# Retention with a gated mixture of attention experts on one core: a tile's value products moved half a step to a step later, the loads of its transposed weights to the head of the step, and its scaling and transposes in among the projections' copies

## The chip, the cores and the metric

The kernel runs on one core of one Trainium2 chip. The metric is the time of one execution on the device, in microseconds (us); the median of several runs is compared.

## What is computed

The first half is a retention layer without softmax, the second a layer of four attention experts of which each token uses two:

```
q, k, v: (8, 8, 576, 64) fp32                                  # batch, heads, tokens, head size
ret[b,h] = (0.125 * q @ k^T * D_h) @ v                          # D_h[i,j] = gamma_h ** (i-j) for i >= j, else 0
x = ret, heads side by side: (8, 576, 512)
w = softmax of the two largest of x @ w_gate (512 x 4)          # per token
for e in 0..3:                                                  # experts, head size 64
    a = causal softmax of 0.125 * (x @ wq[e]) @ (x @ wk[e])^T
    out += w[:, e] * (a @ (x @ wv[e]) @ wo[e])                  # only where e is one of the two
```

## The kernel before

**Steps.** The tokens of a batch are cut into five chunks (`CH`: 128, 128, 128, 128 and 64 rows), so there are 40 chunks (`NC`), and the main loop goes through 42 steps n. Everything is issued in the order in which the code is written: the schedule is manual for all engines, so each engine has one queue in program order and an instruction that waits holds up all that stands behind it. What a step does depends on n mod 5; below, "kind 3" is a step with n mod 5 = 3, and so on.

In step n the kernel (a) issues the loads of chunk n+2 (`load`); (b) does the retention of chunk n: `qk`, the carried state `state`, and with one step of delay `result(n - 1)`, whose matrix products are `old` and `own` and whose elementwise rest (`late`) runs on GpSimd and ScalarE; (c) scores tile m = n - 6 of the second half (`scores`: TensorE products `ss`, then per expert a masked minimum `nm` on VectorE and an exponential on ScalarE); (d) `gates` after a batch's half has its gate logits, `decay` for the next chunk; (e) `normal(m)`: reciprocal row sums on VectorE, then four scalings on ScalarE (L374; two for a tile of kind t = 4); (f) `spread(m)`: VectorE transposes 32x32 blocks (L383) and one DMA writes them to a buffer `hb` in HBM (L386); (g) `work(n)`: projections `pj` (q and k), `pv` (v and gate logits) and `po` (output) of whichever batch is due, by the table `STEPS`; (h) `gather(m)`: four DMAs bring the blocks back as `pth`, now fully transposed (L394); (i) `values(m - 1)`: the products `ys` of the transposed weights with v (L429), copied by ScalarE (`y`, L442) and split into two fp32r parts on GpSimd.

So a tile of place t in its batch (t = 0..4, growing wider with t because of the causal mask) is scored in the step of kind t + 1 (t = 4: kind 0), and its `ys` stands at the end of the next step. Tiles t = 2 and 3 have `pth` loads of 768 KB and 1 MB.

**The table of work.** By n mod 5: kind 3 has the first-half q and k projections (`kq0`, 48 matmuls), kind 4 the output projection `o0` of the batch before (24), kind 0 the values `v0` (24), kind 1 `kq1` (48, wider), kind 2 `o1` and then `v1` (24 and 36).

**PSUM.** All products go to one pool of eight banks (`bank`, tag "b") that are handed out in turn: a new bank waits for the reader of the bank handed out eight before. SBUF has a ring "big" of three buffers for `tr` and the raw weights, and a ring of two for `p32`, the scores.

**DMA.** All transfers are issued by SyncE (SP) in program order, so a `pth` load that waits for its `hb` write to land holds up the loads behind it.

**End.** After step 41 `end()` finishes the last tiles; tiles from LAST + 1 = 36 on are transposed on TensorE (`turn`) instead of through HBM.

Of the kernel before, what the change touches and what calls it, by code (L numbers as in the profile page):

```python
# [34 lines left out]
def kernel(ctx: ExitStack, tc: tile.TileContext, xf, xt, vkf, vkt,  # L35
# [167 lines left out]
    def fetch(n):  # L203
        o, kc, w = WCUT[n]
        RAW[n] = raw = ld.tile([128, kc, w], F32, name="raw", tag="big", bufs=3)
        nc.sync.dma_start(raw, wraw[:, o:o + kc * w].rearrange("p (k w) -> p k w", k=kc))
# [99 lines left out]
    def scores(m):  # L306
# [18 lines left out]
        else:  # L325
            ps = []
            for p in range(2):
                ps.append([bank([128, 288], "ss") for j in range(2)])
                for i in range(2):
                    for z in range(2):  # L330
                        j = i ^ z
                        mm(ps[p][j][HALF[z]], q[p][HALF[z], l0:l0 + C], k[p][HALF[z], 288 * j:288 * j + 288],  # L332
                           start=True, stop=True)
        p32 = sb.tile([128, n, w if t < 4 else 640], F32, name="p32", tag="p32", bufs=2)
        if t == 4:
# [21 lines left out]
    def normal(m):  # L357
        b, t = divmod(m, 5)
        t0, C = CH[t]
        r = 0 if t < 2 else 1  # L360
        ti = t - RNG[r][2][0]
        p32, sm, n = SS[m]
        wt = WT[b, r]
        rs = sm[:, 1, :n]
        v.tensor_scalar(sm[:, 0, :n], sm[:, 0, :n], 1e-9, None, op0=OP.add)
        v.reciprocal(rs, sm[:, 0, :n])
        if t < 4:
            v.tensor_mul(rs, rs, wt[:, ti])  # L368
        else:
            for z in range(2):  # L370
                hr = slice(64 * z, 64 * z + 64)
                v.tensor_mul(rs[hr], rs[hr], wt[hr, ti, z::2])
        for e in range(n):
            act(p32[:, e, :t0 + C], p32[:, e, :t0 + C], AF.Copy, scale=rs[:, e:e + 1])  # L374

    HB = {}

    def spread(m):
        p32, sm, n = SS.pop(m)
        nj = m % 5 + 1  # L380
        tr = ld.tile([128, 4, n, nj, 32], F32, name="tr", tag="big", bufs=3)
        for e in range(n):
            v.transpose(tr[:, :, e].rearrange("p b j c -> p j b c"),  # L383
                        p32[:, e, :128 * nj].rearrange("p (j b c) -> p j b c", b=4, c=32))
        HB[m] = hb = hbm.tile([128, 4, n * nj * 32], F32, name="hb", tag="hb")
# [78 lines left out]
    for b in range(B):  # L464
        late = b == B - 1

        for n, kind in ((5 * b + 3, "kq0"), (5 * b + 5 - late, "v0"), (5 * b + 6, "kq1"), (5 * b + 7, "v1"),
                        (5 * b + 9 + (b == B - 2), "o0"), (5 * b + 12, "o1")):
            if b or kind[-1] == "1" or kind == "o0":
                STEPS.setdefault(n, []).append((b, kind, None))  # L470

# [21 lines left out]

    LAST = NC - 5
    TILES = {n: [n - LAG] for n in range(LAG, NC + 1)}
    TILES[NC].append(LAST)
    TILES[NC + 1] = [LAST + 1]

    def end():
# [6 lines left out]
        gates()  # L506
        normal(LAST + 3)
        run(scores(LAST + 4))
        for d in range(4):
            run(outproj(b - 1, 1, d))  # L510
        run(turn(LAST + 3))
        normal(LAST + 4)
        run(scores(LAST + 2))
        for d in range(4):
            run(outproj(b, 0, d))
        values(LAST + 3)
        run(turn(LAST + 4))
        normal(LAST + 2)
        values(LAST + 4)
        run(turn(LAST + 2))  # L520
# [11 lines left out]
    for n in range(NC + 2):  # L532
# [6 lines left out]
        if n in (1, 4):  # L539
            fetch("v" if n == 1 else "o")  # L540
        new, old = TILES.get(n, []), TILES.get(n - 1, [])
        late = result(n - 1) if 1 <= n <= NC else iter(())
# [15 lines left out]
        soft = scores(new[0]) if new else iter(())  # L558
        turns = (None for m in old if m > LAST for _ in turn(m))
        for i, _ in enumerate(soft):  # L560
            if i:
                next(turns, None)
        if n > 5:
            run(late)
        decay(n + 1)
        run(turns)
# [5 lines left out]
        for m in new:  # L572
            normal(m)
            if m <= LAST:
                spread(m)
        run(work(n))
        for m in new:
            if m <= LAST:
                gather(m)
        run(late)  # L580
        for m in old:
            values(m)
    end()


# [53 lines left out]
```

## Time and profile before

| | |
|---|---|
| median of 3 runs (lowest, highest) | 531.57 us (527.06 to 533.68) |
| profiled execution, its own time | 527.11 us |
| span of that execution, first to last instruction | 525.3 us |
| mean granted TensorE clock | 0.932 |
| TensorE matmul busy | 438.9 us |
| ScalarE / VectorE / GpSimd busy | 298.7 / 291.5 / 214.3 us |
| DMA | 97.38 MB, mean 185 GB/s |

Around the span lie 1.8 us of the profiled time. Durations below come from this one execution. Five steps make one batch; a row of the timeline gives start, duration, engine, line, operation, tiles, shapes and count, and in brackets the idle time of that engine ahead of it with what ended it.

### The profile page before, as it was taken

The page shows a single profiled execution, that of the slowest core. Times are in us where ns is not written, and L with a number is a line of the kernel's source. Part 1 is how long each engine was busy: PE and PEld are TensorE (multiplying, and loading weights), DVE is VectorE, ACT ScalarE, POOL GpSimd, SP SyncE. Part 2 cuts the span into 40 slices and gives each one's busy share as a digit, 9 for nine tenths or more (in the row PEclk, how much of TensorE's full clock was granted, in tenths as well). Part 3 has the DMA queues.
Part 4 walks back from the last instruction along what each step waited for, and adds up shares of the span by engine and source line. Part 5 has one row for each costly group of instructions (what it writes and reads, how often), then busy time and mean ns, then how long its engine had stood idle before and what let it go on. Part 6 is the DMA issues. An engine that isn't in the chain of part 4 may idle for free. (4 is left out here: it accounts for less than half of the span.)

```text
span 525.3 us, 18683 instructions
## 1 busy us (share of the span) xinstructions
PE 438.9 (84%) x7642; PEld 384.2 (73%) x7642; DVE 291.5 (55%) x1050; ACT 298.7 (57%) x886; POOL 214.3 (41%) x285
## 2 busy tenths in 40 slices
PE   6498886699877998789966998689987799587996
PEld 3488775699757896689855997579966798376785
DVE  3646665475744656475655547467565466643451
ACT  2365766356653576447573475645765465836493
POOL 2347444355343443454443453445435354320200
PEclk9599998899977999799998999799998899979899
DMA  8862258756388373865678554875739834456021
GB/s 295 303 201 86 92 182 276 228 158 204 143 265 242 115 235 116 277 210 177 204 237 256 171 176 155 268 230 170 233 118 286 250 116 132 121 161 181 2 81 62
DMA packets 48437, 97.38 MB, mean 185 GB/s; under 512 B 5600, under 2 KB 29408, under 8 KB 47456
## 3 DMA queue, kind: packets, MB, share of 16 engines
q1 hardware_dynamic: 48352, 96.19, 57.7%
q8 instruction: 61, 1.00, 0.8%
q14 instruction: 24, 0.20, 0.1%
HBM read 63.53 MB, written 32.64 MB: 183 GB/s over the span
## 5 line engine op out<-in xcount | busy, mean ns | idle before, releaser
L352 ACT ACTIVATE p<-p,nm 128x128 f32<-128x128 f32 (+4 forms) x144 | 82.9, 578 | 76.4 <-DVE nm L344 57.1
L429 PE MATMUL ys<-pth,vn 128*64 128x128 f32 (+1 forms) x960 | 67.4, 301 | 52.8 <-DMA pth<-hb 36.7
L374 ACT ACTIVATE p<-p,sm 128x128 f32<-128x128 f32 (+4 forms) x144 | 73.0, 575 | 62.7 <-DVE sm L368 51.2
L429 PEld LDWEIGHTS ys<-pth,vn 128*64 128x64 f32 x960 | 57.4, 162 | 59.4 <-DVE tr L383 25.3
L443 POOL CAST yh<-y 128x256 fp32r<-128x256 f32 (+1 forms) x39 | 14.6, 374 | 179.7 <-ACT y L442 179.7
L383 DVE STREAM_TRANSPOSE tr<-p 128x128 f32<-128x128 f32 (+3 forms) x130 | 64.6, 536 | 26.8 <-ACT p L374 17.7
L184 DVE TENSOR_TENSOR x<-x,own 128x256 f32<-128x256 f32 (+1 forms) x80 | 26.4, 363 | 84.5 <-ACT x L169 67.8
L144 POOL TENSOR_SCALAR_AFFINE_SELECT p<-p 64x512 f32<-64x512 f32 (+1 forms) x80 | 49.1, 613 | 30.1 <-ACT p L141 20.6
L344 DVE CUSTOM_DVE_ANT_0 p<-ss,mask 128x512 f32<-128x512 f32 (+3 forms) x128 | 54.9, 484 | 8.9 <-PE ss L323 8.8
L192 POOL TENSOR_TENSOR x1l<-x,x1h 128x512 fp32r<-128x512 f32 (+1 forms) x24 | 26.3, 1097 | 58.3 <-ACT x1h L190 58.3
L189 POOL TENSOR_TENSOR x<-x,gi 128x512 f32<-128x512 f32 (+1 forms) x38 | 44.8, 1180 | 3.4 <-DVE s L126 0.4
L323 PE MATMUL ss<-k,q 64*64 64x512 f32 (+3 forms) x512 | 45.1, 443 | 1.3 <-ACT p L141 0.7
L442 ACT ACTIVATE y<-ys 128x256 f32<-128x256 f32 (+1 forms) x39 | 14.2, 364 | 40.5 <-PE ys L429 40.5
L166 PE MATMUL old<-x,s 64*64 64x64 f32 x1024 | 26.4, 230 | 11.8 <-ACT k L238 10.8
L179 PE MATMUL own<-p,vk 64*64 64x64 f32 x1152 | 29.7, 232 | 5.4 <-issue 3.6
L141 ACT ACTIVATE p<-qk 128x256 f32<-128x256 f32 (+1 forms) x80 | 24.8, 367 | 15.3 <-PE qk L138 15.3
L105 POOL TENSOR_TENSOR vk<-vk,con 128x512 f32<-128x512 f32 (+1 forms) x34 | 32.5, 955 | 0.1
L166 PEld LDWEIGHTS old<-x,s 64*64 64x64 f32 x1024 | 21.8, 144 | 13.4 <-ACT k L238 11.7
L179 PEld LDWEIGHTS own<-p,vk 64*64 64x64 f32 x1152 | 25.8, 145 | 6.1 <-issue 5.2
L138 PE MATMUL qk<-x 64*64 64x64 f32 x1152 | 29.6, 246 | 0.0
L454 PE MATMUL po<-yh,who 128*128 128x320 f32 (+1 forms) x128 | 29.1, 309 | 0.6 <-ACT yh L438 0.6
L138 PEld LDWEIGHTS qk<-x 64*64 64x64 f32 x1152 | 23.9, 154 | 7.5 <-issue 5.5
(113 smaller groups left out, 996.5 us busy)
## 6 DMA issues: line engine op xcount, KB each, us to landing
x<-xf SPq DMA_DIRECT2D x32, 512.0 KB, 5.5
vk<-vkf SPq DMA_DIRECT2D x32, 512.0 KB, 6.3
hb<-tr SPq DMA_DIRECT2D x7, 1024.0 KB, 5.2
pth<-hb SPq DMA_DIRECT2D x28, 256.0 KB, 5.0
hb<-tr SPq DMA_DIRECT2D x7, 768.0 KB, 3.9
pth<-hb SPq DMA_DIRECT2D x28, 192.0 KB, 3.7
out<-ot SPq DMA_DIRECT2D x32, 160.0 KB, 2.7
hb<-tr SPq DMA_DIRECT2D x7, 640.0 KB, 3.8
```

The source lines that it names most:

```text
L105: (gp if n > 5 else v).tensor_mul(vv, vv, gam[:, 2 * c:2 * c + k].unsqueeze(3).to_broadcast([128, k, 4, D]))
L138: mm(ps[g][HALF[r], s, u], x[HALF[g], 1, h, i], x[HALF[g], 0, h, i], start=True, stop=True)
L144: gp.affine_select(w, w, pattern=[[0, 4 * k], [1, 64]], base=0, channel_multiplier=-1, compare_op=OP.is_ge, fill=0.0)
L166: mm(old[g][HALF[u], r, i], S_[b, k - 1][HALF[g], r, u], x[HALF[g], 0, 2 * r + u, i], start=True, stop=True)
L179: mm(own[r][HALF[u], g, i], vk[HALF[r], s, 0, 2 * g + u], p[HALF[r], g, s, u], start=True, stop=True)
L189: e.tensor_mul(x32, x32, gi[:, :, t0:t0 + C])
L323: mm(ps[2 * p + z][HALF[i]], q[p][HALF[z], l0 + 64 * i:l0 + 64 * i + 64], k[p][HALF[z], :w], start=True, stop=True)
L344: v.tensor_tensor_reduce(p32[:, e], ps[e], mask[:, 512 - w:], -1.0, BIG, OP.add, OP.min, nm[:, e:e + 1])
L352: act(p32[:, e, :w], p32[:, e, :w], AF.Exp, bias=bias, scale=-1.0, accum_out=sm[:, 0, e:e + 1])
L374: act(p32[:, e, :t0 + C], p32[:, e, :t0 + C], AF.Copy, scale=rs[:, e:e + 1])
L383: v.transpose(tr[:, :, e].rearrange("p b j c -> p j b c"), p32[:, e, :128 * nj].rearrange("p (j b c) -> p j b c", b=4, c=32))
L429: mm(py[64 * z:64 * z + 64, p], VN[b, rr][0][:, j - 2 * rr, e * D:(e + 1) * D], src, start=(j == 0), stop=(j == t))
```

## The change

It does five things. `values(m)` moves from the end of step m + 7 to the middle of step m + 8, behind the scoring of that step and ahead of `decay`, `gates`, `normal` and `work`. `gather(m)` moves from the end of step m + 6 to the head of step m + 7, behind that step's `load`. The scalings leave `normal` and go into `spread`, which is now a generator: one scaling and one transpose per expert are issued after each piece of `work` from the second on, and the `hb` write after the last of them. The table `STEPS` cuts `kq0` in two, one half each in kinds 3 and 4, and moves `o0` by one step to kind 0; within a step v comes first, then o, then the q and k projections. `p32`, `tr` and the raw weights share one ring of four buffers. At the end the tiles from 34 on (`FAR = LAST - 1`) are transposed on TensorE.

```diff
-        p32 = sb.tile([128, n, w if t < 4 else 640], F32, name="p32", tag="p32", bufs=2)
+        p32 = ld.tile([128, n, w if t < 4 else 640], F32, name="p32", tag="big", bufs=4)
...
-        for e in range(n):
-            act(p32[:, e, :t0 + C], p32[:, e, :t0 + C], AF.Copy, scale=rs[:, e:e + 1])
...
     def spread(m):
-        p32, sm, n = SS.pop(m)
+        t0, C = CH[m % 5]
+        p32, sm, n = SS[m]
         nj = m % 5 + 1
-        tr = ld.tile([128, 4, n, nj, 32], F32, name="tr", tag="big", bufs=3)
+        if m < FAR:
+            tr = ld.tile([128, 4, n, nj, 32], F32, name="tr", tag="big", bufs=4)
         for e in range(n):
-            v.transpose(tr[:, :, e].rearrange("p b j c -> p j b c"),
-                        p32[:, e, :128 * nj].rearrange("p (j b c) -> p j b c", b=4, c=32))
+            act(p32[:, e, :t0 + C], p32[:, e, :t0 + C], AF.Copy, scale=sm[:, 1, e:e + 1])
+            if m < FAR:
+                v.transpose(tr[:, :, e].rearrange("p b j c -> p j b c"),
+                            p32[:, e, :128 * nj].rearrange("p (j b c) -> p j b c", b=4, c=32))
+            yield
+        if m >= FAR:
+            return
+        SS.pop(m)
         HB[m] = hb = hbm.tile([128, 4, n * nj * 32], F32, name="hb", tag="hb")
         nc.sync.dma_start(hb, tr.rearrange("p b e j c -> p b (e j c)"))
...
-        for n, kind in ((5 * b + 3, "kq0"), (5 * b + 5 - late, "v0"), (5 * b + 6, "kq1"), (5 * b + 7, "v1"),
-                        (5 * b + 9 + (b == B - 2), "o0"), (5 * b + 12, "o1")):
+        for n, kind, part in ((5 * b + 3, "kq0", 0), (5 * b + 4 - late, "kq0", 1), (5 * b + 5 - late, "v0", None),
+                              (5 * b + 6, "kq1", None), (5 * b + 7, "v1", None), (5 * b + 10, "o0", None),
+                              (5 * b + 12, "o1", None)):
...
+    for n in STEPS:
+        STEPS[n].sort(key=lambda x: "vok".index(x[1][0]))
...
+    FAR = LAST - 1
...
-        new, old = TILES.get(n, []), TILES.get(n - 1, [])
+        new, old, far = TILES.get(n, []), TILES.get(n - 1, []), TILES.get(n - 2, [])
+        for m in old:
+            if m < FAR:
+                gather(m)
...
         if n > 5:
             run(late)
+        for m in far:
+            if m < FAR:
+                values(m)
         decay(n + 1)
...
         for m in new:
             normal(m)
-            if m <= LAST:
-                spread(m)
-        run(work(n))
-        for m in new:
-            if m <= LAST:
-                gather(m)
+        spreads = (None for m in new for _ in spread(m))
+        for i, _ in enumerate(work(n)):
+            if i:
+                next(spreads, None)
+        run(spreads)
         run(late)
         for m in old:
-            values(m)
+            if m >= FAR:
+                values(m)
```

How the queues read, at three places in the middle of the program. First ScalarE, from the exponentials of a tile t = 2 (step kind 3) to the retention copies of the next step; `p` scaled by `sm` is the scaling, `k` and `q` from `pj` are the copies of the projections, `y` that of the value products. Before:

```order
L352 ACTIVATE p_3302,sm<-p_3302,nm 128x384 x4
L190 ACTIVATE x1h<-x_3227 128x4x128
L294 ACTIVATE ex<-ex 128x12
L374 ACTIVATE p_3302<-p_3302,sm 128x384 x4
L238 ACTIVATE k_3349<-pj 128x256
L240 ACTIVATE q_3351<-pj 128x256
L238 ACTIVATE k_3350<-pj 128x256
L240 ACTIVATE q_3352<-pj 128x256
L442 ACTIVATE y_3423<-ys 128x256
L141 ACTIVATE p<-qk 128x128 x2
L169 ACTIVATE x_3448<-old 128x256 x2
```

ScalarE at the same place now:

```order
L352 ACTIVATE p_3291,sm<-p_3291,nm 128x384 x4
L190 ACTIVATE x1h<-x_3216 128x4x128
L448 ACTIVATE y_3312<-ys 128x256
L294 ACTIVATE ex<-ex 128x12
L383 ACTIVATE p_3291<-p_3291,sm 128x384
L238 ACTIVATE k_3338<-pj 128x256
L383 ACTIVATE p_3291<-p_3291,sm 128x384 x3
L240 ACTIVATE q_3340<-pj 128x256
L141 ACTIVATE p<-qk 128x128 x2
L169 ACTIVATE x_3407<-old 128x256 x2
```

The copy `y` now stands ahead of the gates' exponential, two of the four projection copies have gone to the next step, and one of the other two stands behind the first scaling.

Second TensorE, from the end of a step of kind 4 into one of kind 0; `vn_2101` and `vn_1639` before are the halves of v that tile t = 2 needs. Before:

```order
L454 MATMUL po<-yh_2159,wlo 128x256 x2
L429 MATMUL ys<-pth,vn_1639 64x128 x4
L429 MATMUL ys<-pth,vn_2101 64x128 x2
L429 MATMUL ys<-pth,vn_1639 64x128 x4
L429 MATMUL ys<-pth,vn_2101 64x128 x2
L138 MATMUL qk<-x 64x64 x16
L166 MATMUL old<-x,s 64x64 x8
L179 MATMUL own<-p,vk 64x64 x8
L118 MATMUL st<-vk 64x64 x16
L332 MATMUL ss<-k_1283,q_1842 64x288 x4
L332 MATMUL ss<-k_1284,q_1843 64x288 x4
L257 MATMUL pv<-whv,xh 128x260 x4
```

TensorE now, with the same tile's products:

```order
L233 MATMUL pj<-xh,wlq 128x256 x4
L138 MATMUL qk<-x 64x64 x16
L166 MATMUL old<-x,s 64x64 x8
L179 MATMUL own<-p,vk 64x64 x8
L118 MATMUL st<-vk 64x64 x16
L332 MATMUL ss<-k_1272,q_1831 64x288 x4
L332 MATMUL ss<-k_1273,q_1832 64x288 x4
L435 MATMUL ys<-pth,vn_1592 64x128 x4
L435 MATMUL ys<-pth,vn_2050 64x128 x2
L435 MATMUL ys<-pth,vn_1592 64x128 x4
L435 MATMUL ys<-pth,vn_2050 64x128 x2
L257 MATMUL pv<-whv,xh 128x260 x4
```

The `ys` of tile t = 2 has moved past the retention products and the scores of the next step and stands directly ahead of `pv`.

Third SP's queue, from the loads at the head of a step of kind 3 to the tile t = 3 of kind 4. Before:

```order
L92 DMA x<-xf 128x1024
L96 DMA vk<-vkf 128x1024
L386 DMA hb<-tr 128x1536
L394 DMA pth<-hb 32x4x384 x4
L92 DMA x<-xf 128x1024
L96 DMA vk<-vkf 128x1024
L386 DMA hb<-tr 128x2048
L458 DMA out<-ot 128x256 x4
L394 DMA pth<-hb 32x4x512 x4
```

SP's queue now, from the write of the tile t = 2:

```order
L392 DMA hb<-tr 128x1536
L92 DMA x<-xf 128x1024
L96 DMA vk<-vkf 128x1024
L400 DMA pth<-hb 32x4x384 x4
L392 DMA hb<-tr 128x2048
L92 DMA x<-xf 128x1024
L96 DMA vk<-vkf 128x1024
L400 DMA pth<-hb 32x4x512 x4
L392 DMA hb<-tr 128x1280
```

Each pair of loads `x` and `vk` now stands between a tile's `hb` write and its `pth` loads, and the four `out` writes have left this stretch.

More of the change, by code (lines that the diff above doesn't have):

```diff
@@ L204, in fetch @@
         o, kc, w = WCUT[n]
-        RAW[n] = raw = ld.tile([128, kc, w], F32, name="raw", tag="big", bufs=3)
+        RAW[n] = raw = ld.tile([128, kc, w], F32, name="raw", tag="big", bufs=4)
         nc.sync.dma_start(raw, wraw[:, o:o + kc * w].rearrange("p (k w) -> p k w", k=kc))
@@ L465 @@
         late = b == B - 1
-        for n, kind in ((5 * b + 3, "kq0"), (5 * b + 5 - late, "v0"), (5 * b + 6, "kq1"), (5 * b + 7, "v1"),
-                        (5 * b + 9 + (b == B - 2), "o0"), (5 * b + 12, "o1")):
+        for n, kind, part in ((5 * b + 3, "kq0", 0), (5 * b + 4 - late, "kq0", 1), (5 * b + 5 - late, "v0", None),
+                              (5 * b + 6, "kq1", None), (5 * b + 7, "v1", None), (5 * b + 10, "o0", None),
+                              (5 * b + 12, "o1", None)):
             if b or kind[-1] == "1" or kind == "o0":
-                STEPS.setdefault(n, []).append((b, kind, None))
+                STEPS.setdefault(n, []).append((b, kind, part))
+    for n in STEPS:
+        STEPS[n].sort(key=lambda x: "vok".index(x[1][0]))
     for n, kind, part in ((2, "kq0", 0), (3, "kq0", 1), (4, "v0", 0), (5, "v0", 1)):
@@ L507, in end @@
         normal(LAST + 3)
+        run(spread(LAST + 3))
         run(scores(LAST + 4))
@@ L512, in end @@
         normal(LAST + 4)
+        run(spread(LAST + 4))
         run(scores(LAST + 2))
@@ L518, in end @@
         normal(LAST + 2)
+        run(spread(LAST + 2))
         values(LAST + 4)
@@ L558 @@
         soft = scores(new[0]) if new else iter(())
-        turns = (None for m in old if m > LAST for _ in turn(m))
+        turns = (None for m in old if m >= FAR for _ in turn(m))
         for i, _ in enumerate(soft):
```

## The prediction

> **What bounds the kernel now.** I read first how busy the engines are over the whole span.
>
> ```profile
> PE 438.9 (84%) x7642; PEld 384.2 (73%) x7642; DVE 291.5 (55%) x1050; ACT 298.7 (57%) x886; POOL 214.3 (41%) x285
> ```
>
> TensorE is the fullest engine, and 525.3 - 438.9 = 86 us of it are idle. The view of waits, for TensorE alone, says what ended the idle times (total, times, longest):
>
> ```profile
> PE ys L429 <- DMA pth<-hb: 36.7, 11, 5.1
> PE old L166 <- ACT k L238: 10.8, 7, 1.7
> PE ys L429 <- DVE lg L262: 8.3, 2, 4.2
> PE ys L429 <- DVE tr L383: 7.5, 2, 3.8
> ```
>
> Three of the four are the value products `ys` waiting for their transposed weights: 52.5 us in 15 waits. The names behind the arrow in the third and fourth differ only because several semaphores are waited for; the loads of `pth` follow those transposes. Next, where they sit: one batch in the view by stretches, cut where the scores of a tile start (kinds 3, 4, 0, 1, 2; length, then busy time of the engines, then granted clock, DMA share and GB/s).
>
> ```profile
> 252.84:264.46 11.62, 9.96 (x174) 8.60 (x167) 9.03 (x32) 6.63 (x20) 4.23 (x5) 1.00 0.46 132
> 264.46:277.68 13.22, 9.48 (x176) 7.79 (x169) 6.57 (x19) 9.34 (x26) 7.26 (x10) 0.87 0.90 288
> 277.68:292.50 14.82, 10.36 (x197) 8.83 (x192) 6.93 (x22) 5.36 (x14) 4.67 (x8) 0.88 0.75 218
> 292.50:303.50 11.00, 11.00 (x243) 10.57 (x239) 7.46 (x34) 5.96 (x24) 5.47 (x8) 1.00 0.57 176
> 303.50:315.10 11.60, 11.60 (x227) 10.87 (x220) 5.71 (x25) 8.32 (x26) 6.15 (x8) 1.00 0.53 175
> ```
>
> Two of five stretches (the last two rows) have TensorE busy throughout at full clock, 2.4 GHz; nothing but less TensorE work could shorten them. The idle time lies in the first three, and in the second and third part of the time is at 1.2 GHz. Their waits one by one, in the timeline of TensorE:
>
> ```profile
> 263.42 0.62 PE L166 MATMUL old<-x,s 64*64 64x64 f32 x26 [1.66 <-ACT k L238]
> 273.23 1.95 PE L429 MATMUL ys<-pth,vn 128*64 128x128 f32 x24 [3.74 <-DVE tr L383]
> 277.68 2.11 PE L332 MATMUL ss<-k,q 64*64 64x288 f32 x16
> 287.32 3.22 PE L429 MATMUL ys<-pth,vn 128*64 128x128 f32 x32 [4.46 <-DMA pth<-hb]
> ```
>
> So a batch loses 1.66 us to a bank that the copy of `k` frees late, 3.74 us to tile t = 2 and 4.46 us to tile t = 3. The same three parts over all batches, as sums of stretches of the view: from the scores of t = 2 to those of t = 4 (seven of them), from there to those of t = 0 (six), on to those of t = 2 (six); and the whole middle, six cycles of five steps:
>
> ```profile
> sum 179.70, PE 138.97 PEld 116.93 DVE 108.45 ACT 110.26 POOL 77.22; mean PE 19.85 PEld 16.70 DVE 15.49 ACT 15.75 POOL 11.03
> sum 80.50, PE 60.50 PEld 51.68 DVE 41.77 ACT 32.75 POOL 28.82; mean PE 10.08 PEld 8.61 DVE 6.96 ACT 5.46 POOL 4.80
> sum 137.80, PE 136.47 PEld 129.15 DVE 79.77 ACT 85.93 POOL 70.00; mean PE 22.74 PEld 21.53 DVE 13.29 ACT 14.32 POOL 11.67
> 65.90:438.50 372.60, 317.29 (x5707) 282.18 (x5701) 214.60 (x780) 214.37 (x644) 167.00 (x218) 0.94 0.65 204
> ```
>
> That is 25.7 + 13.4 + 23.0 = 62.1 us a cycle, 372.6 / 6. I call the parts A, B and C, and price the change part by part.
>
> **What TensorE's pieces cost.** Rows at full clock (two of them are shares of one line in a stretch):
>
> ```profile
> 252.84 1.50 PE L323 MATMUL ss<-k,q 64*64 64x384 f32 x16
> 252.84:264.46 11.62, 5.97 (x48) 5.76 (x48) 1.00 0.46 132
> 260.17 1.09 PE L429 MATMUL ys<-pth,vn 128*64 128x128 f32 x16
> 264.46:277.68 13.22, 3.12 (x24) 2.91 (x24) 0.87 0.90 288
> 277.68:292.50 14.82, 3.14 (x24) 2.93 (x24) 0.88 0.75 218
> 300.27 1.39 PE L429 MATMUL ys<-pth,vn 128*64 128x64 f32 x40
> 250.30 0.66 PE L429 MATMUL ys<-pth,vn 128*64 128x128 f32 x8
> 471.24 1.97 PE L429 MATMUL ys<-pth,vn 128*64 128x128 f32 x32 [1.03 <-DMA pth<-hb]
> 515.94 1.53 PE L429 MATMUL ys<-pth,vn 128*64 128x128 f32 x24
> 250.89:252.84 1.95, 1.95 (x131) 1.95 (x133) 0.24 (x2) 1.60 (x5) 1.31 (x3) 1.00 0.99 320
> ```
>
> In order: scores of t = 2; the 48 matmuls of `kq0` (5.97, so 2.98 for a half); `ys` of t = 1; the 24 of `o0` (3.12) and of `v0` (3.14); `ys` of t = 4, 0, 3 and 2; and the retention products of one step (1.95).
>
> **Part C, bound by TensorE.** Kind 1 now computes `ys` of t = 3 in place of t = 4 (+0.58), kind 2 that of t = 4 in place of t = 0 (+0.73). C goes from 23.0 to **24.3**. Scalings and copies there change places on ScalarE, which is busy 14.32 of 22.7 us; I cost that at nothing. If that cover went, a bank freed one copy late would cost what the 1.66 us wait above costs.
>
> **Part B.** It takes over `o0` and has `ys` of t = 2 instead of t = 3. Its pieces: scores of t = 4 2.11, `ys` 1.53, `v0` 3.14, `o0` 3.12, retention 1.95: 11.85, less about 0.5 since each row carries its last matmul's tail beside the next row. So **11.3** instead of 13.4, if nothing is waited for.
>
> **Part A, where order decides.** TensorE's own work there shrinks: scores 1.50, `ys` of t = 0 0.66, half of `kq0` 2.98, retention of kind 4 about 1.5 (no `state` there), scores of t = 3 2.0 (1.50 x 512/384), `ys` of t = 1 1.09, the other half 2.98, retention 1.95: 14.7 us against 25.7 now. It will not run in 14.7, because of ScalarE's queue:
>
> ```profile
> 260.96 2.13 ACT L374 ACTIVATE p<-p,sm 128x384 f32<-128x384 f32 x4 [2.87 <-DVE sm L368]
> 263.00 0.36 ACT L238 ACTIVATE k<-pj 128x256 f32<-128x256 f32 x1
> 264.63 0.69 ACT L169 ACTIVATE x<-old 128x256 f32<-128x256 f32 x2
> 266.09 0.68 DVE L344 CUSTOM_DVE_ANT_0 p<-ss,mask 128x512 f32<-128x512 f32 x1
> 270.45 2.56 ACT L374 ACTIVATE p<-p,sm 128x512 f32<-128x512 f32 x4 [0.19 <-DVE sm L368]
> ```
>
> The first scaling of t = 2 starts 8.1 us after its scores, because the gates and row sums come first on VectorE; the moved copy `y` ahead of them adds about 0.3. The `k` copy then follows one scaling instead of four, but the `q` copy still follows the fourth: 252.84 + 8.4 + 2.13 + two copies of about 0.3 = 264.0. Counting eight banks back in the new order, the first two score banks of t = 3 are those of this `k` and `q`. So TensorE, ready at about 259.5, gets the first at 262 and the second at 264.0: the new wait of some 4.5 us, with the scores behind it, takes the place of the old one at `old`. The masked minimum of t = 3 starts at 266, as now; its scalings at 270.2 end, with `k` between, at 273.1, and the `q` copy at 273.4 frees a `state` bank of kind 0. From there 0.5 us to the scores of t = 4: A is 21.1 at least, and 22.5 if the projections run at half clock and their copies come late. I take **21.6**; the ends are 14.7 (if banks don't tie TensorE to ScalarE) and 25.7 (nothing gained).
>
> **The transfers.** Each step's `x` and `vk` loads now stand between the `hb` write and the `pth` loads.
>
> ```profile
> 267.05 1.75 SPq L394 DMA_DIRECT2D pth<-hb  x4
> 268.90 0.38 SPq L92 DMA_DIRECT2D x<-xf  x1
> 273.78 0.33 SPq L386 DMA_DIRECT2D hb<-tr  x1
> 279.39 1.89 SPq L394 DMA_DIRECT2D pth<-hb  x4
> ```
>
> ```profile
> x<-xf SPq DMA_DIRECT2D x32, 512.0 KB, 5.5
> ```
>
> For t = 3: write issued at 273.78, `pth` loads at 279.39, `ys` starts at 287.32, 7.9 us on. After, the write goes out at about 274.0; the products are wanted after the scores of t = 0, at 252.84 + 21.6 + 11.3 + 0.6 = 286.3. If the loads cost nothing, `pth` is there at 287.3 or, without the four `out` writes beside it, about a microsecond earlier. At worst they cost one `x` landing, 5.5 us. I take 0.4 us of waiting; the range is 0 to 5.5. Tile t = 2 (`pth` issued 267.05, used at 273.23) is wanted only at 276.5, 3 us later than it is there now. The others are smaller and have more than 20 us.
>
> The row first: `pth` loads at 267.05 went out ahead of `x` at 268.90 and had the engines to themselves. The Trainium skill, "DMA: Bandwidth & Descriptors", section "Queues, rings and completion order", says that each DMA engine consumes its descriptors in ring order; this speaks against the change, since loads issued ahead would be read ahead of `pth`. By that rule `pth` would come late by what is left of the loads when it is issued. The trace of before has no `pth` load behind a pair of loads, so nothing in it decides this.
>
> **The end.** After the last cycle 86.8 us are left (525.3 - 438.5).
>
> ```profile
> 460.25 2.15 PE L429 MATMUL ys<-pth,vn 128*64 128x128 f32 x17 [5.09 <-DMA pth<-hb]
> 484.71 1.66 PE L429 MATMUL ys<-pth,vn 128*64 128x64 f32 x41 [2.15 <-DMA pth<-hb]
> ```
>
> These two waits go: the first since its tile is wanted later, the second since tile 34 is now transposed on TensorE. But `ys` of tile 33 comes to stand ahead of `kq1` and its `pth`, which came 22.9 us after the scores in the batch above (264.46 to 287.32), is waited for instead. Between -7.2 and 0 I take -3.
>
> **Sum.** A cycle: 21.6 + 11.3 + 24.3 + 0.4 = 57.6 instead of 62.1; six of them -27, the end -3. The profiled execution took 527.1 us; so 497. It lies 0.8% under the median of 531.57, and the same share gives **500 us**.
>
> **Rivals.**
> 1. *Late transfers.* The loads ahead delay `pth` of t = 3 by 2 us more than assumed: a cycle is 59.6, the sum 527 - 15 - 3 = 509, median 513. For it: DMA share 0.90 and 288 GB/s in the second stretch. Against: the loads are issued while SP still waits for the write, so they may be through. Chance 0.18.
> 2. *Slower, by the same place.* `ys` now stands ahead of a step's projections, and its copy `y` ahead of the step's scalings, so a late `pth` stops both queues. With the full 5.5 us and 2 us for half clock (the stretch of 14.82 us at 0.88 has 3.6 us of it, which cost 1.8), a cycle is 57.6 + 7.5 = 65.1: +18 and -3, 542, median 547. It decides from 4.5 us of delay on. Against: `pth` of t = 2 has 3 us to spare and the smaller tiles more. Chance 0.04.
> 3. *ScalarE keeps the pace.* The copies, spread between scalings, free the banks no earlier, and A stays near 25.7 while C grows by 1.3: a cycle 61.7, 527 - 2 - 3 = 522, median 526: the change moves waits and not the end. Chance 0.06.
> 4. *More comes back.* TensorE runs ahead of ScalarE in A, which becomes 18, and no clock is lost: a cycle of 54 gives 527 - 49 - 3 = 475, median 479. For it: 14.7 us of work there; against: the second bank. Chance 0.10. The Trainium skill, "TensorE: Matmul & The Clock Gate", section "Terms", prices throttled time at the time times one less the granted share; by that formula a mean clock of 0.932, 71 us at half, would be worth 36 us. I don't add it: in A, TensorE waits for ScalarE anyway.
>
> My forecast has the other 0.62, with 488 to 509 as its own range (A from 21.1 to 22.5, 0 to 1.5 us for `pth`, the end). The range is **486 to 515**; beyond it lie the slower rival, most of rivals 3 and 4. A measurement of this kernel can tell about 2% from no change, 521 to 542. Faster: forecast, rival 4 and most of rival 1, 0.87; within 2%: 0.09; slower: 0.04.
>
> **What would show it.** Right: no wait of `ys` over 1.5 us in kinds 4 and 0; a wait of 3 to 5 us at the scores of t = 3, ended by the `q` copy; A 21 to 22.5, B 11 to 12, C 24 to 24.6; the `old` wait for `k` gone. Wrong: `ys` still ended by `pth` in kinds 0 or 1 (rivals 1, 2), or A at 25 (3) or under 19 (4). The forecast fails if the bank count is wrong or the loads hold `pth` up.

## The result, and the profile after

The changed kernel takes 508.27 us (median of four runs, 505.58 to 509.51) against 530.0 us for the kernel before (four runs, one more than in the table ahead of the prediction, 527.06 to 533.68). The ratio is 0.958, with a 95% interval of 0.950 to 0.966: 4.2% faster. The profiled execution took 509.51 us, with a span of 507.7 us and a mean granted clock of 0.933; before it was 527.11, 525.3 and 0.932. The span is 17.6 us shorter and the mean clock is the same. Here and below a median is over all runs of a kernel, a ratio over its fast runs alone, without those more than 1.5% above its fastest.

First the engines of the changed kernel over the span (busy us, share, instructions).

```profile
PE 448.5 (88%) x7656; PEld 377.0 (74%) x7656; DVE 284.1 (56%) x1048; ACT 303.6 (60%) x890; POOL 213.4 (42%) x285
```

TensorE was idle for 86 us of the span and is now idle for 59 (507.7 - 448.5). Its busy time rose from 438.9 to 448.5 with only 14 more instructions (the transposes of tiles 34 and 35), so a part of the idle time has become longer rows, at the scores of t = 3 above all (below): the matmuls of L323 are busy for 63.6 us, 45.1 before. Next TensorE's view of waits in the changed kernel (total, times, longest).

```profile
PE ss L323 <- ACT k L238: 16.7, 6, 2.9
PE ys L435 <- DMA pth<-hb: 7.0, 4, 2.6
PE st L118 <- POOL vk L105: 5.6, 8, 1.2
PE ys L435 <- ACT p L352: 5.5, 3, 2.0
```

Before, `ys` waited 52.5 us in 15 waits; now 7.0 + 5.5 = 12.5 us in 7. (The second name is again that of another semaphore: the last `pth` load of those three landed 0.1 to 0.3 us ahead of the products.) The 10.8 us at `old` are gone, and 16.7 us at the scores of t = 3 are new. One batch in the view by stretches, cut as in the prediction, at the scores of t = 2, 3, 4, 0, 1 and 2; behind it the sums over six cycles of A, B and C, and the middle and the end.

```profile
246.70:256.00 9.30, 6.45 (x141) 5.07 (x130) 7.18 (x29) 4.35 (x14) 5.01 (x7) 0.99 0.67 174
256.00:268.40 12.40, 11.75 (x154) 7.13 (x156) 8.39 (x21) 10.28 (x28) 5.68 (x8) 0.73 0.74 213
268.40:279.50 11.10, 11.10 (x215) 9.82 (x208) 6.51 (x23) 6.74 (x19) 5.08 (x9) 1.00 0.99 280
279.50:292.60 13.10, 11.69 (x239) 11.11 (x232) 7.17 (x34) 6.67 (x24) 6.18 (x8) 1.00 0.91 285
292.60:304.90 12.30, 12.30 (x259) 11.61 (x252) 5.53 (x25) 8.25 (x25) 5.57 (x8) 1.00 0.35 122
...
sum 129.80, PE 107.83 PEld 72.92 DVE 93.27 ACT 87.86 POOL 64.12; mean PE 17.97 PEld 12.15 DVE 15.54 ACT 14.64 POOL 10.69
sum 66.70, PE 66.70 PEld 59.01 DVE 38.98 ACT 40.52 POOL 30.59; mean PE 11.12 PEld 9.83 DVE 6.50 ACT 6.75 POOL 5.10
sum 159.20, PE 147.73 PEld 139.32 DVE 75.48 ACT 89.40 POOL 70.89; mean PE 24.62 PEld 23.22 DVE 12.58 ACT 14.90 POOL 11.81
...
66.40:422.10 355.70, 322.26 (x5704) 271.24 (x5697) 207.72 (x780) 217.78 (x643) 165.60 (x217) 0.94 0.72 214
422.10:507.70 85.60, 74.26 (x805) 61.18 (x796) 41.09 (x160) 52.18 (x148) 18.30 (x31) 0.94 0.27 79
```

| us per cycle | before | forecast | measured |
|---|---|---|---|
| A (scores of t = 2 to those of t = 4) | 25.7 | 21.6 | 129.80 / 6 = 21.6 |
| B (on to those of t = 0) | 13.4 | 11.3 | 66.70 / 6 = 11.1 |
| C (on to those of t = 2), with the wait for `pth` | 23.0 | 24.3 + 0.4 | 159.20 / 6 = 26.5 |
| cycle | 62.1 | 57.6 | 355.70 / 6 = 59.3 |
| end | 86.8 | 83.8 | 85.6 |

A and B came out as forecast, B with TensorE busy all the time (66.70 of 66.70). C did not. Where A and C have their waits stands in TensorE's timeline: three places of the batch above, the scores of t = 3 of a later batch (there the profile keeps the second bank's matmuls apart), and the `ys` of t = 3 in two earlier batches and at the end (start, duration, in brackets the idle time ahead).

```profile
255.98 5.47 PE L323 MATMUL ss<-k,q 64*64 64x512 f32 x16 [2.85 <-ACT k L238]
375.63 3.42 PE L323 MATMUL ss<-k,q 64*64 64x512 f32 x14 [0.71 <-ACT q L240]
267.85 0.69 PE L118 MATMUL st<-vk 64*64 64x64 f32 x32 [0.65 <-POOL vk L105]
281.51 1.97 PE L435 MATMUL ys<-pth,vn 128*64 128x128 f32 x32 [1.41 <-DMA pth<-hb]
102.00 3.55 PE L435 MATMUL ys<-pth,vn 128*64 128x128 f32 x32 [2.00 <-DMA pth<-hb]
162.47 2.62 PE L435 MATMUL ys<-pth,vn 128*64 128x128 f32 x32 [2.04 <-ACT p L352]
457.45 3.48 PE L435 MATMUL ys<-pth,vn 128*64 128x128 f32 x32 [2.60 <-DMA pth<-hb]
```

The scores of t = 3 wait twice, for `k` and, inside the longer row, for `q`, as forecast; 14 of their matmuls then take 3.42 us. The products of t = 3 wait for `pth` in every batch (2.0, 2.0, 1.8, 1.4, 1.7 and 1.0 us, mean 1.65). In the two batches with 2.0 us, half clock followed and cost 1.6 us more: in the first all of it in the products, 3.55 instead of 1.97 us, in the second in the products (2.62) and the first two rows of `kq1` behind them. That is seen in the six stretches C of the changed kernel, of which two stand below the others in granted clock:

```profile
99.36:127.35 27.99, 25.85 (x480) 24.29 (x475) 12.70 (x60) 14.96 (x49) 12.12 (x16) 0.94 0.62 190
159.79:188.09 28.30, 25.82 (x482) 24.26 (x476) 12.45 (x59) 15.04 (x49) 11.78 (x15) 0.94 0.59 182
220.90:246.66 25.76, 24.00 (x481) 22.74 (x476) 12.38 (x59) 14.94 (x49) 11.77 (x15) 1.00 0.63 202
279.46:304.89 25.43, 24.02 (x483) 22.75 (x477) 12.74 (x59) 14.95 (x49) 11.78 (x15) 1.00 0.64 206
337.68:364.53 26.85, 24.21 (x482) 22.71 (x476) 12.45 (x59) 14.93 (x49) 11.81 (x15) 1.00 0.61 195
397.07:422.10 25.03, 24.00 (x481) 22.73 (x474) 12.95 (x59) 14.71 (x49) 11.79 (x15) 1.00 0.65 203
```

TensorE's own work in C at full clock is 24.0 to 24.2 us, as the sum had it (24.3).

ScalarE's timeline in the changed kernel, where part A waits for it:

```profile
255.05 0.61 ACT L383 ACTIVATE p<-p,sm 128x384 f32<-128x384 f32 x1 [2.81 <-DVE sm L368]
255.57 0.36 ACT L238 ACTIVATE k<-pj 128x256 f32<-128x256 f32 x1
255.83 1.61 ACT L383 ACTIVATE p<-p,sm 128x384 f32<-128x384 f32 x3
257.35 0.37 ACT L240 ACTIVATE q<-pj 128x256 f32<-128x256 f32 x1
```

The first scaling starts 8.4 us after the scores (255.05 - 246.66), the first bank comes free with `k` at 9.3, and the `q` copy ends at 11.1. The forecast had 8.4, 9.2 and 11.1. And SP's queue, from the write of t = 3 to its loads:

```profile
268.06 0.34 SPq L392 DMA_DIRECT2D hb<-tr  x1
268.44 0.97 SPq L92 DMA_DIRECT2D x<-xf  x1
272.60 1.75 SPq L400 DMA_DIRECT2D pth<-hb  x4
```

In this batch, write to loads takes 4.5 us (5.6 before) and loads to products 8.9 (272.60 to 281.51; 7.9 before): 13.45 us now and 13.54 before. Over all six batches the means are 5.0 us (5.2 before) and 8.7 (8.0 before), 13.7 against 13.25. So the path without the `out` writes gave 0.2 us, and with the loads of `x` and `vk` ahead the way from loads to products grew by 0.7.

### The profile page after: what moved, and what is told of

Read it like the earlier page. It is cut to its first block, busy times and chain, and to the rows that moved or that the text cites. A ratio compares the mean times of both kernels' runs of the same rounds, so it can differ in the third digit from the quotient of the medians.

```text
span 507.7 us, 18675 instructions
## 1 busy us (share of the span) xinstructions
PE 448.5 (88%) x7656; PEld 377.0 (74%) x7656; DVE 284.1 (56%) x1048; ACT 303.6 (60%) x890; POOL 213.4 (42%) x285
## 4 chain that ended last, share of the span: by engine, by line
PE 53%; ACT 18%; DVE 11%; DMA 9%; POOL 4%; issue 3%; SPq 1%; DVEq 0%; ACTq 0%; POOLq 0%
PE pj L233 11%; PE po L460 9%; PE pv L257 8%; PE ss L323 8%; PE ys L435 7%; ACT p L352 7%; DMA pth<-hb 5%; ACT p L383 4%; DMA hb<-tr 3%; PE qk L138 2%; DVE s L126 2%; PE ss L332 2%; ACT x1h L190 2%; ACT p L141 2%; DVE p L344 2%
## 5 line engine op out<-in xcount | busy, mean ns | idle before, releaser
L352 ACT ACTIVATE p<-p,nm 128x128 f32<-128x128 f32 (+4 forms) x144 | 82.9, 578 | 75.4 <-DVE nm L344 59.3
L383 ACT ACTIVATE p<-p,sm 128x128 f32<-128x128 f32 (+4 forms) x144 | 76.6, 578 | 51.5 <-DVE sm L368 45.4
L385 DVE STREAM_TRANSPOSE tr<-p 128x128 f32<-128x128 f32 (+4 forms) x124 | 64.2, 542 | 30.9 <-ACT p L383 25.0
L323 PE MATMUL ss<-k,q 64*64 64x512 f32 (+3 forms) x512 | 63.6, 530 | 18.2 <-ACT k L238 16.7
L435 PEld LDWEIGHTS ys<-pth,vn 128*64 128x64 f32 x960 | 50.6, 149 | 37.0 <-ACT p L352 16.4
L435 PE MATMUL ys<-pth,vn 128*64 128x128 f32 (+1 forms) x960 | 59.9, 279 | 14.0 <-DMA pth<-hb 7.0
L344 DVE CUSTOM_DVE_ANT_0 p<-ss,mask 128x512 f32<-128x512 f32 (+3 forms) x128 | 55.4, 486 | 13.4 <-PE ss L323 13.2
L323 PEld LDWEIGHTS ss<-k,q 64*64 64x64 f32 x512 | 23.3, 150 | 38.5 <-ACT k L238 17.5
L463 ACT ACTIVATE ot<-po 128x256 f32<-128x256 f32 (+1 forms) x64 | 25.4, 408 | 18.3 <-PE po L460 17.9
L141 ACT ACTIVATE p<-qk 128x256 f32<-128x256 f32 (+1 forms) x80 | 24.5, 359 | 12.1 <-PE qk L138 12.1
L118 PE MATMUL st<-vk 64*64 64x64 f32 x1024 | 23.4, 226 | 7.8 <-POOL vk L105 5.6
L192 POOL TENSOR_TENSOR xl<-x,xh 128x512 fp32r<-128x512 f32 x14 | 18.0, 1286 | 27.3 <-ACT xh L190 27.3
L450 POOL TENSOR_TENSOR yl<-y,yh 128x256 fp32r<-128x256 f32 (+1 forms) x39 | 26.4, 676 | 3.1
```

The lines of the kernel that those rows point to most:

```text
L192: e.tensor_sub(xl[:, :, l0:l0 + C], x32, f(xh[:, :, l0:l0 + C]))
L323: mm(ps[2 * p + z][HALF[i]], q[p][HALF[z], l0 + 64 * i:l0 + 64 * i + 64], k[p][HALF[z], :w], start=True, stop=True)
L344: v.tensor_tensor_reduce(p32[:, e], ps[e], mask[:, 512 - w:], -1.0, BIG, OP.add, OP.min, nm[:, e:e + 1])
L352: act(p32[:, e, :w], p32[:, e, :w], AF.Exp, bias=bias, scale=-1.0, accum_out=sm[:, 0, e:e + 1])
L383: act(p32[:, e, :t0 + C], p32[:, e, :t0 + C], AF.Copy, scale=sm[:, 1, e:e + 1])
L385: v.transpose(tr[:, :, e].rearrange("p b j c -> p j b c"), p32[:, e, :128 * nj].rearrange("p (j b c) -> p j b c", b=4, c=32))
```

## The experiments

Four theories were to be told apart: (1) the later products remove waits for transfers, (2) the interleaved scalings free banks earlier, (3) the cut of `kq0` shortens A, and (4) what is missing from the forecast is lost at `pth` of t = 3. The kernels were run in three groups, each beside the kernel before on one chip (medians 530.7, 529.39 and 526.06 us); a ratio is to that group's runs of it.

**The products back at the end of step m + 7.** Everything else is as in the changed kernel.

```diff
-        for m in far:
-            if m < FAR:
-                values(m)
...
         for m in old:
-            if m >= FAR:
-                values(m)
+            values(m)
```

> The changed kernel, but the value products of a tile stand at the end of the step after its scoring again; table, loads and scalings stay as changed. Theory (the later place of the products is what removes the waits): the products of t = 2 wait at the end of kind 4 for about 6 us and those of t = 3 at the end of kind 0 for 1 to 2 us, a cycle of five steps goes from 59.3 back to about 62 us, and the time to about 527 us, as before the change. Rival (the table of work or the order on ScalarE brings the gain): within 1% of the changed kernel, about 508 us.

It took 553.84 us, ratio 1.034 (1.022 to 1.046): slower than the kernel before. The part A, 21.6 us in the changed kernel, is 27.5 here. TensorE's view of waits:

```profile
PE ys L435 <- DMA pth<-hb: 71.0, 18, 7.1
```

The waits for `pth` are back, some three in a batch, and the longest is longer than before (5.1), since the `pth` loads now go out only at the head of the step at whose end they are wanted. In the six cycles it is the tiles t = 1, 2 and 4 that wait in nearly every batch, and t = 3, expected to wait 1 to 2 us, in one alone. The direction was as the theory says, the size larger by some 21 us, by the ratio. The products half a step to a step later are what makes room for the gather at the head of the step; that gather without them is a loss. The later products with the gather at its old place were not run.

**Scalings and transposes ahead of the projections.**

```diff
-        spreads = (None for m in new for _ in spread(m))
-        for i, _ in enumerate(work(n)):
-            if i:
-                next(spreads, None)
-        run(spreads)
+        for m in new:
+            run(spread(m))
+        run(work(n))
```

> The changed kernel, but all scalings and transposes of a step stand ahead of its projections again. Theory (in kinds 3 and 4 the second copy, behind the fourth scaling, sets the pace in either order): within 1% of the changed kernel, 503 to 513 us, the stretch from the scores of t = 2 to those of t = 4 still 21 to 22 us. Rival (a first copy behind one scaling instead of four is what frees TensorE): about 1.7 us a cycle lost, 518 us.

504.14 us, ratio 0.946 (0.938 to 0.955). TensorE's waits at the scores of t = 3:

```profile
PE ss L323 <- ACT k L238: 26.0, 6, 4.4
```

The wait for the `k` copy grows from 2.9 to 4.4 us, and A stays at 21.45 us. So the interleaving takes 1.5 us off a wait that was not the end of anything. It delays the last transpose, though: without it the write of t = 3 goes out 20.9 us after the scores of t = 2 instead of 21.3 (means over six batches), and `pth` of t = 3 is waited for 0.7 to 1.9 us, 1.2 on average, instead of 1.65. Whether the kernel is truly faster than the changed one is not decided, as the intervals overlap.

**The old table of work, unsorted.** `kq0` whole in kind 3, `o0` back in kind 4, o ahead of v.

```diff
-        for n, kind, part in ((5 * b + 3, "kq0", 0), (5 * b + 4 - late, "kq0", 1), (5 * b + 5 - late, "v0", None),
-                              (5 * b + 6, "kq1", None), (5 * b + 7, "v1", None), (5 * b + 10, "o0", None),
+        for n, kind, part in ((5 * b + 3, "kq0", None), (5 * b + 5 - late, "v0", None), (5 * b + 6, "kq1", None),
+                              (5 * b + 7, "v1", None), (5 * b + 9 + (b == B - 2), "o0", None),
...
-    for n in STEPS:
-        STEPS[n].sort(key=lambda x: "vok".index(x[1][0]))
```

> The changed kernel with the old table of work (48 projections in kind 3, the output projection o0 in kind 4). Theory (the chain from the scores of t = 2 through those of t = 3 to its landed weights sets a cycle, about 35 us, and the 24 us behind it are TensorE's): the 3 us that leave kind 0 turn into a longer wait for pth of t = 3 in kind 1, 4 to 5 us instead of 1.7, and the time stays within 1.5%, 503 to 516 us. Rival (TensorE's work per step decides): 3 us a cycle in either direction, under 492 or over 525 us.

584.40 us, ratio 1.100 (1.093 to 1.107), outside every expectation. TensorE's view of waits names the largest part of the reason:

```profile
PE po L460 <- POOL yh L449: 47.9, 12, 4.5
```

With the products in the middle of the step, an output projection in the same step's `work` stands directly behind them and waits for their copy on ScalarE and their split on GpSimd: 4 us, twelve times, once in kind 4 and once in kind 2 of each cycle. That is 8 of the 12.5 us by which a cycle grew (71.8 against 59.3). The wait for `pth` of t = 3 rose to 4.0 us on average, as the theory had it, and is 2.3 of them. In the changed kernel v stands between the two in kind 2, and `o0` has a step more. The prediction spoke of the table only as work moved from A to B; that it is also the cover of the split of `y` had not been seen.

**The gather ahead of the loads of `x` and `vk`.** The loop that calls `gather` moves above `load(n + 2)`.

> The changed kernel with the pth loads issued ahead of the step's x and vk loads. Theory (the loads ahead hold up pth of t = 3, which took 8.2 us from its issue in the changed kernel and 7.3 us before): pth lands about 0.9 us earlier, the wait of about 1.7 us in kind 1 falls to under 1 us, no half clock behind it, a cycle loses 1 to 1.5 us, about 500 us. Rival (pth is late because its tile is scored and written late): the wait stays, within 0.5% of the changed kernel.

516.16 us, ratio 0.969 (0.961 to 0.977). This theory fell. The DMA rows of t = 3, first in the changed kernel, then in this one (KB of one, median us from issue to landing):

```profile
hb<-tr SPq DMA_DIRECT2D x7, 1024.0 KB, 5.2
pth<-hb SPq DMA_DIRECT2D x28, 256.0 KB, 6.6
```

```profile
hb<-tr SPq DMA_DIRECT2D x7, 1024.0 KB, 5.7
pth<-hb SPq DMA_DIRECT2D x28, 256.0 KB, 5.1
```

Once out, the loads landed 1.5 us sooner, and the write 0.5 later. But `pth` of t = 3 was used 25.6 us after its tile's scores on average (25.0 to 26.6 in six batches), against 25.7 (24.9 to 26.2) in the changed kernel, and waited for 1.63 us on average, against 1.65: nearly nothing was gained on the whole way from scores to products. What made this kernel slower stands in its waits:

```profile
PE ys L435 <- DMA pth<-hb: 7.8, 5, 2.7
PE ys L435 <- ACT p L352: 4.7, 2, 3.0
PE ys L435 <- issue: 4.1, 1, 4.1
PE ss L323 <- issue: 3.7, 1, 3.7
```

The first two are as in the changed kernel (12.5 us together, here too). The last two are new, 7.8 us in two idle times, both in kind 2, for which the view names nothing. The trace of the DMA packets has a candidate: a load of 16 KB of instructions (queue q8 of the page) starts in both, at 173.31 and 296.67, and TensorE goes on 2.4 and 2.2 us after that start; the last section has the same for the other runs. The four cycles without such an idle time of over 1 us take 58.0 to 60.7 us, as in the changed kernel (57.6 to 61.0). Why the instructions are loaded so late in just these two is not shown.

**The products of t = 3 behind `kq1`.** Timed beside a second run of the changed kernel on the same chip (505.85 us, ratio 0.957, 0.950 to 0.964).

```diff
         for m in far:
-            if m < FAR:
+            if m < FAR and (m % 5 != 3 or m == 33):
                 values(m)
...
         run(spreads)
+        for m in far:
+            if m < FAR and m % 5 == 3 and m != 33:
+                values(m)
         run(late)
```

> The changed kernel again, beside the next three on the same chip: 505 to 510 us.

> The changed kernel, but the value products of tiles t = 3 stand behind the projections of kind 1 instead of ahead of them (tile 33 excepted). Theory (what a cycle takes beyond the forecast is the wait for pth of t = 3 in kind 1 and the half clock after it): no wait of these products, the stretch from the scores of t = 0 to those of t = 1 back to 12 to 12.5 us, a cycle 57 to 57.8 us instead of 59.3, about 497 us. Rival (the excess lies elsewhere in kinds 1 and 2): the time stays within 0.7% of the changed kernel.

497.0 us, ratio 0.940 (0.932 to 0.948), below the changed kernel's interval. The theory held in the cycle. By stretches, the scores of t = 0 to those of t = 1 summed over six cycles, and the middle:

```profile
sum 72.80, PE 70.65 PEld 66.83 DVE 45.83 ACT 38.33 POOL 38.30; mean PE 11.78 PEld 11.14 DVE 7.64 ACT 6.39 POOL 6.38
...
65.00:411.60 346.60, 316.66 (x5703) 268.44 (x5696) 210.52 (x780) 216.53 (x643) 165.61 (x217) 0.96 0.73 219
```

The first is 12.1 us (72.80 / 6) where the changed kernel has 14.06, and 13.4 in its second profile, beside this one. The cycle is 346.60 / 6 = 57.8 (59.3 and 58.9), almost the forecast's 57.6; A is unchanged at 21.5. In that second profile the products of t = 3 wait 1.3 to 2.35 us, and no half clock follows, not even behind the longest of these waits:

```profile
159.12 1.97 PE L435 MATMUL ys<-pth,vn 128*64 128x128 f32 x32 [2.35 <-DMA pth<-hb]
```

So the wait for `pth` of t = 3 is what the forecast had missed in a cycle; the half clock behind it came on top in two batches of the first profile alone. Not all of the gain lies there: between the two profiles on this chip the six cycles give 6.5 us and the end 2.6, where `pth` of tile 33, whose products stand where they stood, is waited for 1.46 us instead of 3.38.

**The projections' copies ahead of the scalings**, in kinds 3 and 4 alone (`run(work(n))` ahead of `spread`). It asks whether the score banks set A.

> The changed kernel, but in kinds 3 and 4 the projections' copies stand ahead of the four scalings on ScalarE. Theory (the pace there is ScalarE's queue as a whole: the retention copies of the next step, on which VectorE's masked minimum waits, stand behind the scalings in any order): the scores of t = 3 start some 2 to 4 us earlier but the stretch from the scores of t = 2 to those of t = 4 falls by no more than 1 us, to 20.6 to 21.6, and the time stays within 1%. Rival (the two score banks that the late copies free set the pace): that stretch falls to 17 to 18.5 us, the time to 485 to 492.

505.5 us, ratio 0.948 (0.940 to 0.956). The first two banks came 3 us sooner, the scores of t = 3 began 6.35 us after those of t = 2 (9.28 in the changed kernel), but their second half waited up to 3.4 us more, and those of t = 4 came 14.78 us after that beginning (12.33): A is 21.1. TensorE's waits:

```profile
PE ss L323 <- ACT p L141: 20.3, 8, 3.4
```

The wait has only moved to another copy of ScalarE's queue. A is therefore set by the chain through VectorE and ScalarE as a whole, not by the two banks that the prediction counted.

**Three edits together**: the scalings ahead, the products of t = 3 behind `kq1`, and `decay` ahead of the products.

> The changed kernel with three edits: scalings and transposes ahead of the projections, the value products of t = 3 behind the projections of kind 1, and decay ahead of the value products (so GpSimd does it ahead of the split of y). Theory: pth of t = 3 a microsecond earlier but no longer waited for, the wait of state for decay in kind 0 (about 1 us) gone: a cycle 56 to 57 us, 489 to 494 us. Rival (one of the edits only moves its wait): 497 us or more.

497.58 us, ratio 0.940 (0.935 to 0.945): no better than the second of the three alone, and short of the expected 489 to 494. The `state` products of kind 0 still wait for GpSimd, now by the name of the split of `y` (2.3 us in four waits, the longest 0.8), and the stretch of kind 2 is 13.1 us on average instead of 12.5, with `decay` ahead of the split that its output projection needs. The direction is the rival's; no row shows all of the 0.6 us.

**`kq0` whole in kind 3**, the rest of the table as changed (one entry with `None` instead of the two halves).

> The changed kernel with kq0 in one piece again, 48 matmuls in kind 3 and no projection in kind 4; the rest of the table (v ahead of o, o0 in kind 0) stays. Theory (ScalarE's and VectorE's chain from the scores of t = 2 to those of t = 4 sets that stretch, wherever the projections' copies stand in it): it stays at 21 to 22.5 us and the time within 1% of the changed kernel. Rival (the cut in two is what shortens it): back to 24 us or more, 520 us or more.

506.01 us, ratio 0.964 (0.958 to 0.970), A 22.1 us: the cut brings half a microsecond in A, and no more than that in a cycle (59.5 against 59.3). TensorE's waits show where the removed work went:

```profile
PE st L118 <- POOL vk L105: 29.3, 8, 5.2
```

Without the half of `kq0` in kind 4, TensorE stands at `state` of kind 0 for GpSimd's `decay` instead, up to 5.2 us.

**The gates at the end of the step that makes their logits.** The prediction had said that the first scaling is late because the gates come first on VectorE. Here they leave that place.

```diff
         run(turns)
-        gates()
...
         run(spreads)
+        gates()
```

> The changed kernel with the gates of a half computed at the end of the step that makes their logits (kinds 0 and 2) instead of in the middle of the next one. Theory (the gates stand inside the chain that sets the stretch from the scores of t = 2 to those of t = 4): the first scaling of t = 2 starts 5.5 to 6 us after its scores instead of 8.4, the stretch falls by 2 to 3 us to 18.5 to 19.5, pth of t = 3 comes earlier by as much, a cycle 56 to 57 us, about 491 us. Rival (the gates only move their delay to kind 2): within 1% of the changed kernel.

484.37 us, ratio 0.923 (0.917 to 0.929). TensorE's timeline in one batch of this kernel, from the scores of t = 2, then ScalarE's, and last the sum of A over six cycles and the middle, by stretches:

```profile
178.07 1.47 PE L323 MATMUL ss<-k,q 64*64 64x384 f32 x16
186.18 1.94 PE L323 MATMUL ss<-k,q 64*64 64x512 f32 x14 [0.71 <-ACT q L240]
...
183.47 0.62 ACT L383 ACTIVATE p<-p,sm 128x384 f32<-128x384 f32 x1
185.77 0.36 ACT L240 ACTIVATE q<-pj 128x256 f32<-128x256 f32 x1
```

```profile
sum 108.20, PE 90.88 PEld 68.39 DVE 75.87 ACT 86.75 POOL 64.47; mean PE 15.15 PEld 11.40 DVE 12.64 ACT 14.46 POOL 10.74
...
67.30:400.10 332.80, 307.83 (x5686) 266.25 (x5689) 196.35 (x784) 218.33 (x645) 166.13 (x217) 0.98 0.77 227
```

The first scaling starts 5.4 us after the scores instead of 8.4, and A is 108.20 / 6 = 18.0. The 14 matmuls of the scores of t = 3 take 1.94 us instead of 3.42, and the granted clock of the middle is 0.98 instead of 0.94. The gain is larger than expected (18.5 to 19.5 for A, about 491 us). Part of it goes back in B, 12.0 us: in each batch `state` of kind 0 now waits 2.2 us for GpSimd's `decay`, and in three of the six the scores of t = 4 behind it run longer, 3.3 to 3.8 us instead of 2.1. This shows the step of the prediction that explains A: three microseconds of gates ahead of the scalings, at TensorE's cost.

**With the products of t = 3 behind `kq1` as well.**

> The changed kernel with the early gates and with the value products of t = 3 behind the projections of kind 1. Theory: both gains add in part, since the early gates also bring pth of t = 3 earlier: 484 to 490 us. Rival: no better than the better of the two alone.

479.07 us, ratio 0.911 (0.903 to 0.918): with the next one the fastest of the study, 9% under the kernel before. The cycles do not show the gain: six take 333.1 us here and 332.8 without the second edit. It lies at the end, where `pth` of tile 33 is waited for 1.11 us instead of 3.21 and its products take 1.97 us instead of 3.63. Why `pth` comes earlier there stays open.

**And the scalings ahead of the projections.**

> The same with all scalings and transposes ahead of the projections too. Theory: TensorE waits longer for the first score bank of t = 3 and not at all for the second, the stretch is the same, so within 1% of the kernel with two edits. Rival: 5 us or more apart from it.

478.97 us, ratio 0.911 (0.904 to 0.918). The interleaving brings nothing here either.

## Why the prediction was right, and where a term was off

The forecast was 500 us; the median is 508.27. The path of the gain was as described, and one term was too small. That the miss came out no larger than 8 us is in part luck (below).

- **A, 21.6: right, for a reason that holds only in part.** The waits of t = 2 left it, as the products moved back show (A 27.5). The time of the first scaling, the first bank and the `q` copy came within 0.2 us. The wait at the scores of t = 3 is 3.6 us in all, within the 3 to 5 of the prediction, but 2.85 of it is ended by the `k` copy and 0.71 by the `q` copy that it named. That the gates set it is shown (A 18.0 without them ahead). That the second bank binds is not: TensorE's last wait in A was for GpSimd's `decay`, 0.65 us at 267.85, and with the first two banks free 3 us earlier A was still 21.1. Several queues end within a microsecond of each other there.
- **B, 11.3: right** (11.1). The sum of pieces with nothing waited for was enough, and `pth` of t = 2 was there in time.
- **C, 24.3: right for TensorE's own work** (24.0 to 24.2 at full clock).
- **The transfers, 0.4: the mis-sized term.** The wait for `pth` of t = 3 is 1.65 us, and in two of six batches half clock behind it cost 1.6 us, 0.5 a cycle: 2.2 in place of 0.4. (With TensorE's own 24.1 and 0.2 of idle time without a named releaser that is the 26.5 of C.) The step that failed is the one that let the missing `out` writes bring `pth` about a microsecond earlier and the loads ahead cost next to nothing: from write to loads the six batches gained 0.2 us, and from loads to products they lost 0.7. (The 274.0 of the prediction and the 13.5 us of its rows also make 287.5, not 287.3.) By the prediction's own sign, `ys` ended by `pth` in kind 1, this is the rival of late transfers, and a cycle of 59.3 is nearly that rival's 59.6. With the wait hidden it is 57.8.
- **The end, -3: measured -1.2.** The two named waits went, but `pth` of tile 33 was waited for 2.60 us, and its products ran at half clock (3.48 us).
- **Against the 497 of the sum**: 6 x 1.7 for the cycles, 1.8 for the end and 0.5 ahead of the first cycle make 509.5, the profiled execution's time. The step from there to a median by the share of before's (0.8% more, which gives 501; the prediction took 500) went the wrong way, as this profiled execution was the slowest of its four; that offset 4 us of the miss by luck.
- **The slower rival** needed 4.5 us of delay in a cycle; 2.35 us was the longest wait there in the two profiles of the changed kernel.
- **The rule of the Trainium skill** ("DMA: Bandwidth & Descriptors", "Queues, rings and completion order"), by which loads issued ahead are read ahead of `pth`: the trace agrees in direction, with 0.7 of 8.7 us over six batches. It alone would have misled on the remedy, since the gather put first brought the products earlier by no more than about 0.2 us on the way from scores to products.

Not foreseen was how much the products' place, the gather's place and the table need each other. By the ratios, the products moved back cost some 40 us against the changed kernel (1.034 and 0.958), the table moved back 75 (1.100). The interleaving and the cut of `kq0` are worth nothing that these runs can tell. The ring of four buffers and the two tiles more that TensorE transposes at the end were not tried alone.

## What to carry to other kernels

When a product is moved later to give its transfer time, look for what is queued behind it that reads its result, and move that too: here the output projections, which otherwise wait 47.9 us in all. A wait at a bank in a ring often only shows which of several nearly equal chains ended last; take one element out of the head of the chain (the gates) rather than reorder its tail. And a short wait for a transfer on a path bound by TensorE costs its full length, and now and then, as in two of the twelve batches profiled here, nearly as much again through the clock behind it; so hide it behind other matmuls even where it seems too small to matter.

## What the hardware showed that was not expected

- Half clock in a stretch that waits for another engine cost next to nothing there. In the changed kernel, part A by stretches in three batches:

```profile
188.09:209.77 21.68, 18.34 (x293) 12.24 (x286) 15.57 (x49) 14.61 (x42) 10.68 (x15) 0.84 0.71 194
246.66:268.36 21.70, 18.20 (x294) 12.20 (x286) 15.58 (x49) 14.62 (x42) 10.69 (x15) 0.84 0.71 196
364.53:385.96 21.43, 16.65 (x294) 11.52 (x287) 15.59 (x49) 14.54 (x42) 10.68 (x15) 0.92 0.71 198
```

  The granted clock is 0.84 in two and 0.92 in the third, TensorE's busy time 18.3 and 16.65 us, and the stretch 21.4 to 21.7. In C, where TensorE is the bound, 0.94 against 1.00 went with 1.1 to 3.3 us, the waits for `pth` included.
- Two waits of 2.0 us ahead of `ys` were followed by half clock; one of 2.35 us at the same place, in the second profile of the same kernel, was not. So the length of the wait alone does not tell it.
- Reading 1 MB back from HBM took 1.5 us longer behind 1 MB of other loads than ahead of them (6.6 and 5.1), and in the order that reads it first, the write ahead of it took 0.5 us longer.
- Where TensorE stood idle with nothing named that it waited for, a load of instructions had just begun. The packets in the traces have 61 loads of 16 KB on queue q8 in an execution. All 54 such idle times of 0.3 us or more, in the 14 profiles, end 2.2 to 3.2 us after the start of one (53 of them 2.2 to 2.8); of all matmuls of the changed kernel 11% begin 2.1 to 3.2 us after one. That TensorE waits for its instructions there is the reading that fits; the trace does not say which engine a load is for. The same matmul can meet it with 0.44 us of idle time in one profile of the changed kernel, 1.11 in the other, and 4.14 with the gather put first.
